# One third of a batch transposed on TensorE instead of by DMA, and a new order of loads and work in a fused attention and GEGLU kernel

## The chip, the cores and the metric

The kernel runs on one core of a Trainium2 chip. Its time is the device time of one execution in microseconds (us). Three executions of the kernel before took 412.22, 412.31 and 412.85 us; the median, 412.31 us, is the time before. A core has the engines TensorE (PE: matrix products; its weight loads are listed as PEld), VectorE (DVE), ScalarE (ACT), GpSimd (POOL) and SyncE (SP), each with its own queue of instructions that is worked off in order. POOL and SP issue transfers (DMAs), which 16 DMA engines carry out.

## The reference

Attention without softmax, then a gated feed-forward block, in float32:

```python
batch, n_heads, seq, head_dim = (8, 12, 448, 64)
scores = scale * np.matmul(q, k.transpose(0, 1, 3, 2))
attn = np.maximum(scores, 0.0) ** 2 / S
attn_out = np.matmul(attn, v)
x = attn_out.transpose(0, 2, 1, 3).reshape(B * S, H * D)     # 3584 x 768
g, val = x @ w_gate, x @ w_val                               # 768 -> 1536
gelu = 0.5 * g * (1.0 + erf(g * inv_sqrt2))
out = gelu * val @ w_out                                     # 1536 -> 768
```

## The kernel before, in words

The eight batches are numbered 0 to 7, so the third batch is number 2. A batch's 12 heads are worked in three thirds of four heads (two pairs of heads); the third m of batch b is written (b, m) here and in the code.

**Loads.** POOL issues all loads, and they turn float32 into bf16 on the way. A third of q and one of k go into one tile `qk16` (from a ring of two buffers), a third of v, in two overlapping halves, into `v16` (a ring of three). The gate and value weights come in six column blocks each, `wg[i]` and `wv[i]` (`load_w12`, L410), the output weights in four row blocks `wo[i]` (`load_wo`, L417). A load into a ring waits until the old contents of its buffer have been used. Since POOL issues in order, a load that waits holds all those behind it. In the built program a load also waits for the landing of the one eight places before it, with whose completion semaphore it shares a number. Loads of later batches have one more wait: for a relu instruction of an earlier third (`PACE`, "behind"). In the kernel before, the order of loads is written out as calls at the end of the function: batch 0; weight block 0; third (1, 0); then blocks 1 to 5 between the other thirds of batch 1; then q and k of (2, 0) and (2, 1), v of (2, 0), all four blocks of `wo`, and the remaining thirds, v one third behind q and k.

**Transposes.** The scores need q and k with the head dimension on the partitions (tile `qkT`, a ring of three). For batches 0 and 1 TensorE transposes them with an identity matrix into PSUM (`add_transposes`, products `<-ident,qk` at L641, 28 for each third) and DVE copies the result to `qkT` (two copies, L645). For batches from 2 on (`EARLY = 2`), DVE regroups the third into a tile `qkr` (L477, a ring of two) and SP issues two DMA transposes of `qkr` into `qkT` (L482). Some of these wait for the landing of the one before.

**Attention and feed-forward.** A score unit multiplies into PSUM, ACT applies relu (L708), DVE squares two units at once (L717), and a value unit of each head pair multiplies with v into `xT`. For batches 0 and 1 and some blocks of the others, gate and value products are plain: ACT takes the Gelu (L1002), DVE multiplies (L1007). For blocks 0 to 2 of later batches, two batches together are computed with seven products in place of eight (Winograd's form), and so is the output product, with sums of weights (`ws`, `wt`) and of tokens made on DVE. Nearly all products of TensorE are of 64 x 64 tiles, of which four run beside each other, issued by one helper (L375).

**The order.** The work of TensorE after the first batch is a list of units, named by the string `LINE`: `s` is the next score (or transpose) unit, `o` the next value unit, a digit the next gate or value unit of that batch, `2B4` a product of a pair of batches, `g2` one of the output's groups. At build time `run_plan` plays through all engines with assumed costs: at each step it takes, from the next 60 units of the list, the one that can start first; ACT, DVE and SP take what is ready first. The instructions are emitted in this order, so every engine's order is fixed when the kernel is built. The plan knows when a load lands by adding sizes over an assumed rate; it gives every DMA transpose a landing 5 us after its issue.

Of the kernel before, what the change touches and what calls it, by code (L numbers as in the profile page):

```python
# [9 lines left out]


LINE = """
0 1 4A1 s 1 s 1 0 o 2 5 1 1 o d1 s 4C5 1 1 1 0 o 0 0 c5 s 2C1 s s o 3 s 0 s a1 s 0 1 2B4 o 5 2 g2
o s 3 0 2 b7 s 1 o 6B6 o s s s a5 a7 s 4B1 2 d4 s 0 0 0 0 o s 0 a2 4D1 2C7 s s s o 2E1 2A5 0 2C6 s
2A6 0 0 0 0 b5 0 s s 2 0 s 1 0 s s 1 a6 4E5 d7 2B1 2E2 1 0 o g6 1 f1 s 1 a4 c4 s s 4A2 1 b6 s s
2B6 s s 1 2D3 s o s s o d3 o c2 6B1 s s s 1 s s s 1 b2 s s b1 s s 1 s 3 1 s 2D6 1 c7 a3 s s 2E3 o
f5 o o 2E6 1 g7 1 2F1 b4 s 2B2 s 2A3 b3 2B3 c1 s o s 2F2 4 s s i5 3 c3 4F5 s s c6 s 2 2E7 2C3 2
2B5 2D1 s s 2F3 e6 2B7 s s s 2 3 2 s 2A1 2 6F4 g4 2A2 s 2A7 4E4 s 2A4 s o s s 4 e4 3 o d5 s s o
2D7 2D4 4A5 2C5 o 2D2 s o h2 2C2 2F6 s 2F7 2E5 s 5 f6 2D5 j2 2 4 4A4 4F6 s s 2C4 2F5 e2 s s 5 s
2F4 o 3 o 3 6B5 2E4 h4 2 s 4C1 m6 3 s 3 d6 s 6B2 s 4 3 s s n2 f3 f4 s o d2 o 3 4B4 4A7 6E1 s s e1  # L20
6B7 e7 o o 4B3 g1 s 7 4 6D6 s o f2 s e3 s 6E3 s 5 e5 s 4 6D3 7 m3 4D4 4E7 s m4 f7 s s 4 m5 4A6 s s
5 4 4B6 s 4B2 s s g5 i1 4C2 o o s s 4D2 4 4 s j5 s s j3 j1 s 6C6 g3 5 i7 6 s k5 6A2 o 4B7 s 4F2 5
4D5 4C6 4E2 4E1 s s 4B5 4A3 s s 4D3 s 4E6 6C7 4C3 s 6C3 o 4F3 6A1 4C7 s 4D6 s n1 l4 o s 6A7 s 4 k3
4C4 6 s o h1 4E3 i3 4D7 s h7 6A6 6E7 6 i4 s 4F1 j6 6 o 4 4F4 s n3 s 5 4F7 s i6 s s n5 s s 6D1 6 s
5 h6 s 5 o s 6A5 7 7 6D2 o s s 5 s h5 l7 6 s s 6C4 s n7 s 6E4 6A3 s o 6C1 6E6 i2 o 6E2 7 j7 7 s h3
l5 s s s 6B3 s l1 j4 s 7 6F2 6 s 6C2 k6 o k7 6 6F1 6D7 m7 6B4 7 6A4 6 6 m1 6F7 6 n6 6F6 k4 l2 6E5
m2 l6 k1 6 6D4 7 7 l3 7 7 6C5 6F3 6D5 6F5 n4 k2
"""


class Op:

    def __init__(self, engine, cost, emit, deps=(), lag=0.0, prio=0, other=None):
        self.engine, self.cost, self.emit, self.prio = engine, cost, emit, prio
        self.deps = [d for d in deps if d is not None]
        self.lag = lag
        self.other = other
        self.takes = None
        self.margin = 0.0
        self.after = None  # L40
        self.gates = []
        self.start = self.end = None
        self.place = 0
        self.open = False

# [45 lines left out]
AHEAD = 60  # L91
BANK = 0.3
SPARE = 1


def run_plan(queues, pools, units, banks, arrivals, together, fill):

    free = {e: 0.0 for e in (*queues, *pools)}
    at = {e: 0 for e in queues}
    dma = last = floor = busy = 0.0  # L100
# [11 lines left out]
        for d in before:  # L112
            users.setdefault(d, []).append(op)
    able = {e: [] for e in pools}
    known = {}

    def offer(op):
        t = 0.0 if op.after is None else op.after.start
# [20 lines left out]

    def ready(op):  # L140
        t = known.get(op)
        if t is not None and op.takes is not None:
            x = op.takes[0].free(*op.takes[2:])
            return None if x is None else max(t, x)
        return t
# [63 lines left out]
    while left:  # L209
        best = None  # L210
        for e, ops in queues.items():
            if at[e] < len(ops):
                r = ready(ops[at[e]])
                if r is not None:
                    t = max(r, free[e], floor if e in together else 0.0)
# [23 lines left out]
        if isinstance(op, tuple):  # L239
            _, u, k = op  # L240
# [16 lines left out]
            op = u.los[0]  # L257
# [10 lines left out]
        if op in arrivals:  # L268
            dma = max(dma, op.end) + arrivals[op]
            op.lag = dma + 2.0 - op.end  # L270
        if e in at:
            at[e] += 1
        else:
            for x in homes[op]:
                able[x].remove(op)
# [13 lines left out]
def kernel(  # L289
# [18 lines left out]
    SC = S // P  # L308
    VC = (SC + 1) // 2
    NPAIR = H // 2  # L310
    NM = NPAIR // 2
# [11 lines left out]
    WOG = 3  # L323
# [2 lines left out]
    FB = 4  # L326
    FILL = 30.0
    EARLY = 2
    WO_AT = 2, 2, 2, 2

    NP = 3
    RING_V, RING_T, RING_H, RING_L, RING_A, RING_O, RING_E = 3, 3, 2, 2, 4, 4, 5
# [49 lines left out]
    ACT, DVE, POOL, SP, IDLE = [], [], [], [], []  # L382
    arrivals = {}
# [22 lines left out]
    def load_w12(i):  # L406
        cols = slice(i * WCH, (i + 1) * WCH)

        def emit(wt, src):
            return nc.gpsimd.dma_start(  # L410
                wt[:, :, :], src[:, cols].rearrange("(c p) f -> p c f", p=128))
        w12_op[i] = [load(4 * d_model * WCH, lambda wt=wt, src=src: emit(wt, src))
                     for wt, src in ((wg[i], moe_w_gate), (wv[i], moe_w_val))]

    def load_wo(i):
        rows = slice(i * WOG * 128, (i + 1) * WOG * 128)
        wo_op[i] = load(4 * WOG * 128 * d_model, lambda: nc.gpsimd.dma_start(  # L417
            wo[i][:, :, :], moe_w_out[rows, :].rearrange("(c p) f -> p c f", p=128)))

    def load_qk(b, i, h0, h1, deps=()):  # L420

# [28 lines left out]
            for pr in range(h0 // 2, h1 // 2):  # L450
                head_op[b, pr, 2 + i] = op

    def load_heads(b, h0, h1):
        load_qk(b, 0, h0, h1)
        load_qk(b, 1, h0, h1)
        load_v(b, h0, h1)

    qkT, tr_op = {}, {}

    def qkT_tile(b, m):  # L460
# [5 lines left out]
    one = []  # L466

    def add_dma_transposes(b, m, deps=()):


        wait = Op("IDLE", 2.0 if b == EARLY else 5.0, lambda: None,
                  [*deps] + [head_op[b, pr, i] for pr in (2 * m, 2 * m + 1) for i in range(2)])
        IDLE.append(wait)

        def emit_copy():
            qkr[b, m] = lpool.tile([128, SC, 4, D], bf16, name="qkr", tag="qkr")
            nc.vector.tensor_copy(  # L477
                qkr[b, m].rearrange("p c h d -> p h c d"),
                qk16[b, m].rearrange("p h (c d) -> p h c d", d=D))

        def emit_transpose(c0, c1):
            ins = nc.sync.dma_start_transpose(  # L482
                qkT_tile(b, m)[:, c0:c1].rearrange("d c r x -> d (c r) x"),
                qkr[b, m][:, c0:c1].rearrange("p c h d -> p (c h d)"))
            if b > EARLY and c0 or m and b == EARLY:
                tc.add_manual_dep(ins.ins, one[0].ins.name, SYNC, reason="pace")
            one[:] = [ins]

        n = len(regrouped)
        copy = Op("DVE", 0.62, emit_copy, [wait, *(regrouped[n - RING_L] if n >= RING_L else ())], lag=0.15, prio=1)  # L490
        DVE.append(copy)
        copy.margin = 3.0
        tr_op[b, m] = [Op("SP", 0.19 * 2 * (c1 - c0), lambda c0=c0, c1=c1: emit_transpose(c0, c1),
                          [copy], lag=5.0) for c0, c1 in ((0, VC), (VC, SC))]
        qk_used[b, m] = [copy]
        t_made[b, m] = [*tr_op[b, m]]
        if m or b > EARLY:
            tr_op[b, m][1].deps.append(tr_op[b, m][0])
        if m and b == EARLY:
# [171 lines left out]
    def add_scores(at, b, u):  # L671
# [44 lines left out]
            part = slice(u % 2, u % 2 + 1) if alone else slice(0, 2)  # L716
            nc.vector.tensor_tensor(a[:, part], a[:, part], a[:, part], op=ALU.mult)  # L717

        if b < EARLY:
            have = [t for pr in prs for t in ([t_op[b, m, pr % 2]] if (b, pr) != (0, 0) else t_op[0, 0])]  # L720
        else:
            have = tr_op[b, m]
# [516 lines left out]
        if h0 > 2:  # L1239
            load_v(0, h0 - 4, h1 - 4)  # L1240
    load_v(0, 8, 12)
    load_w12(0)
    load_heads(1, 0, 4)
    load_w12(1)
    load_qk(1, 0, 4, 8)
    load_qk(1, 1, 4, 8)
    load_w12(2)
    load_v(1, 4, 8)
    load_qk(1, 0, 8, 12)
    load_qk(1, 1, 8, 12)  # L1250
    load_w12(3)
    load_v(1, 8, 12)
    load_w12(4)
    load_w12(5)
    late = [(b, m) for b in range(2, B) for m in range(NM)]
    for n, (b, m) in enumerate(late):
        for i in range(FC // WOG):
            if WO_AT[i] == n:
                load_wo(i)
        for i in range(2):  # L1260
            load_qk(b, i, 4 * m, 4 * m + 4)
        for b_, m_ in late[n - 1:n] + (late[n:] if n == len(late) - 1 else []):
            load_v(b_, 4 * m_, 4 * m_ + 4)
    add_weight_sums()
    for b, m in late:
        add_dma_transposes(b, m)


    FINAL = B * SC // 4 - 1
# [199 lines left out]
```

## Time and profile before

The profiled execution took 411.88 us, 0.43 us under the median; its span from the first to the last instruction is 410.1 us.

| what | profiled execution before |
|---|---|
| time, span | 411.88 us, 410.1 us |
| PE busy, products | 392.3 us (96%), 8477 |
| DVE busy | 298.5 us (73%) |
| ACT busy | 244.8 us (60%) |
| POOL busy | 74.1 us (18%) |
| mean granted clock of TensorE | 0.985 |
| DMA: loads' queue, SP's queue (share of 16 engines) | 46.3%, 24.1% |
| DMA transposes | 36, 5.3 us to landing (median) |

Busy time of PE is the time in which any product runs; with four tiles beside each other a busy PE need not be a full one. A wait's line names the waiting group, what ended the wait, the total, the number and the longest of the waits. A line of the timeline gives start, duration, engine, source line, operation, names, shapes and count. The windows give busy time of PE, PEld, DVE, ACT and POOL with counts, then the granted clock (1.00 is full), the mean share of the 16 DMA engines and GB/s.

### The profile page before, as it was taken

How to read it: one execution, taken by the hardware profiler on the slowest of the kernel's cores; microseconds unless marked ns; L12 is line 12 of the kernel's file. 1: busy time of each engine (PE TensorE's matmuls, PEld its weight loads, DVE VectorE, ACT ScalarE, POOL GpSimd, SP SyncE). 2: the span in 40 equal slices, each digit the busy share in tenths (PEclk: the TensorE clock that was granted, in tenths of full speed). 3: DMA queues.
4: the chain of work that ended last, by engine and by line, in shares of the span. 5: the costliest groups of instructions: out<-in, count | busy, mean ns of one | idle time of the engine just before them, and what ended most of it. 6: DMA issues, size and time to landing. Idle time of an engine off the chain costs nothing.

```text
span 410.1 us, 18547 instructions
## 1 busy us (share of the span) xinstructions
PE 392.3 (96%) x8477; PEld 348.1 (85%) x8480; DVE 298.5 (73%) x513; ACT 244.8 (60%) x366; POOL 74.1 (18%) x120
## 2 busy tenths in 40 slices
PE   7999996499999999999999999999999999999994
PEld 3566785399989899989998999999999999989993
DVE  2976776198677978788877777688998766577562
ACT  5947783167677667786666676677776733242220
POOL 7756350111212211110111111111110000000000
PEclk9999999599999999999999999999999999999999
DMA  8999999987899799636498987765331411000245
GB/s 108 190 200 197 198 206 180 122 103 105 131 124 136 119 192 154 93 49 71 56 136 127 158 169 116 122 63 81 54 48 42 118 42 40 4 3 3 65 113 136
DMA packets 75278, 44.84 MB, mean 109 GB/s; under 512 B 36160, under 2 KB 71744, under 8 KB 75200
## 3 DMA queue, kind: packets, MB, share of 16 engines
q0 software_dynamic: 37152, 24.39, 46.3%
q1 hardware_dynamic: 37888, 19.08, 24.1%
q8 instruction: 66, 1.08, 1.1%
q10 hardware_dynamic: 160, 0.20, 0.1%
q14 instruction: 12, 0.10, 0.1%
HBM read 48.76 MB, written 11.01 MB: 146 GB/s over the span
## 4 chain that ended last, share of the span: by engine, by line
PE 91%; DMA 5%; ACT 1%; issue 1%; DVE 1%; SPq 0%; POOL 0%; POOLq 0%
PE ff L375 80%; PE sp L375 8%; DMA qkT<-qkr 4%; PE ff L562 1%; ACT attnT L708 1%; PE sp L641 1%; DMA qk<-in_k_dram 1%; PE ff L641 0%; DVE qkT L645 0%; DVE attnT L717 0%; PE ff L604 0%; ACT gel L1002 0%; DVE osb L1196 0%; SPq L482 0%; ACT qkT L612 0%
## 5 line engine op out<-in xcount | busy, mean ns | idle before, releaser
L375 PE MATMUL ff<-xT,wg 64*64 64x448 bf16 x1872 | 195.4, 351 | 0.0
L708 ACT ACTIVATE attnT<-sp 128x896 bf16<-128x896 f32 x168 | 151.6, 922 | 55.8 <-PE sp L375 53.4
L375 PE MATMUL ff<-xT,wv 64*64 64x448 bf16 x1440 | 156.3, 352 | 0.2 <-issue 0.2
L375 PEld LDWEIGHTS <-wv 64*64 64x64 bf16 x1872 | 115.3, 107 | 8.6 <-issue 0.9
L375 PEld LDWEIGHTS <-wg 64*64 64x64 bf16 x1872 | 113.7, 107 | 9.0 <-issue 0.2
L717 DVE TENSOR_TENSOR attnT<-attnT 128x1792 bf16<-128x1792 bf16 (+1 forms) x98 | 92.3, 953 | 12.6 <-ACT attnT L708 11.9
L375 PE MATMUL sp<-qkT 64*64 64x448 bf16 (+1 forms) x768 | 79.7, 330 | 10.1 <-DMA qkT<-qkr 9.0
L375 PEld LDWEIGHTS <-s 64*64 64x64 bf16 x1344 | 80.2, 107 | 4.4
L375 PE MATMUL ff<-attnT,v 64*64 64x448 bf16 (+1 forms) x768 | 83.7, 326 | 0.1
L375 PE MATMUL ff<-wo,s 64*64 64x384 bf16 x672 | 60.9, 323 | 0.0
L375 PE MATMUL ff<-wt,s 64*64 64x384 bf16 x672 | 60.8, 323 | 0.0
L1007 DVE TENSOR_TENSOR uT<-gel,ff 128x448 bf16<-128x448 bf16 x60 | 37.0, 617 | 31.2 <-PE ff L375 27.0
L375 PEld LDWEIGHTS <-uT 64*64 64x64 bf16 x912 | 55.2, 107 | 2.1
L375 PEld LDWEIGHTS <-qkT 64*64 64x64 bf16 x768 | 39.4, 106 | 16.5 <-issue 7.5
L445 POOL DMA_DIRECT2D v<-in_v_dram x48 | 29.5, 619 | 128.6 <-ACT attnT L708 98.2
L375 PE MATMUL ff<-ts,wv 64*64 64x448 bf16 x432 | 51.5, 349 | 0.0
L375 PE MATMUL ff<-ts,ws 64*64 64x448 bf16 x432 | 51.1, 349 | 0.0
L375 PEld LDWEIGHTS <-v 64*64 64x64 bf16 x768 | 46.9, 106 | 4.0 <-issue 1.0
L375 PE MATMUL ff<-wo,uT 64*64 64x384 bf16 x576 | 49.9, 323 | 0.0
L1002 ACT ACTIVATE gel<-ff 128x448 bf16<-128x448 f32 x60 | 32.5, 544 | 27.0 <-PE ff L375 26.9
L375 PEld LDWEIGHTS <-ws 64*64 64x64 bf16 x648 | 41.1, 106 | 2.3
L924 DVE TENSOR_TENSOR part<-ff,part 128x448 f32<-128x448 f32 x54 | 32.9, 620 | 11.8 <-PE ff L375 7.0
(60 smaller groups left out, 374.7 us busy)
## 6 DMA issues: line engine op xcount, KB each, us to landing
out_dram<-osb SPq DMA_DIRECT2D x54, 192.0 KB, 3.6
v<-in_v_dram POOLq DMA_DIRECT2D x48, 128.0 KB, 3.9
qk<-in_q_dram POOLq DMA_DIRECT2D x23, 224.0 KB, 4.9
qk<-in_k_dram POOLq DMA_DIRECT2D x23, 224.0 KB, 5.9
wg<-in_moe_w_gate_dram POOLq DMA_DIRECT2D x6, 384.0 KB, 10.3
wv<-in_moe_w_val_dram POOLq DMA_DIRECT2D x6, 384.0 KB, 11.2
wo<-in_moe_w_out_dram POOLq DMA_DIRECT2D x4, 576.0 KB, 13.5
qkT<-qkr SPq DMA_TRANSPOSE x36, 5.3
```

The lines of the kernel that those rows point to most:

```text
L375: return nc.tensor.matmul(o, lhsT, rhs, start=start, stop=stop, skip_group_check=onto, tile_position=(P * row, P * col))
L445: return nc.gpsimd.dma_start(v16[b, m][HALF[i], :, :, :], v[b, h0:h1].rearrange("h (p c) d -> p h c d", c=SC)[:, :, c0:c0 + VC, :])
L562: nc.tensor.matmul(t[:, :], warm[:, 0:128], warm[:, :], start=True, stop=True)
L641: nc.tensor.transpose(t[HALF[j], c, :], src[:, 2 * r + j, c, :], ident[:, :], tile_position=(0, P * j))
L708: relu.ins = nc.scalar.activation(duo["a"][:, u % 2, :, :], box[0][:, :, 0:S], AF.Relu).ins
L717: nc.vector.tensor_tensor(a[:, part], a[:, part], a[:, part], op=ALU.mult)
L924: rd.ins = nc.vector.tensor_tensor(t[:, :], box[0][:, 0:S], t[:, :], op=ALU.add).ins
L1002: nc.scalar.activation(gel[b, fc][:, :], box[0][:, 0:S], AF.Gelu)
L1007: u_op[b, fc].ins = nc.vector.tensor_tensor(uT[b][:, fc, :], gel.pop((b, fc))[:, :], box[0][:, 0:S], op=ALU.mult).ins
```

## The change

Three things change, and the order of nearly everything with them.

1. The third (2, 0) is transposed on TensorE (`ON_PE`): 28 more products with the identity and two DVE copies out of PSUM; one `qkr` copy and two DMA transposes less. The others of batch 2 and all later ones stay with DMA.
2. The loads follow a string `LOADS`. After batch 0 it has q, k and v of (1, 0) before weight block 0, then q and k of (1, 1), block 1, v of (1, 1), all of (1, 2), q and k of (2, 0), blocks 2 and 3, q and k of (2, 1), block 4, `wo[0]`, q and k of (2, 2) and (3, 0), v of (2, 0), (2, 1) and (2, 2), block 5, v of (3, 0), and so on; `wo` comes as 0, 2, 1, 3, spread out.
3. `LINE` is a new list. The plan's assumptions change too: rates of the weight loads, at most eight loads in flight (`FLIGHT`), and the time that a DMA transpose takes of the DMA engines (`queued`). These act only at build time, through the order.

```diff
 LINE = """
-0 1 4A1 s 1 s 1 0 o 2 5 1 1 o d1 s 4C5 1 1 1 0 o 0 0 c5 s 2C1 s s o 3 s 0 s a1 s 0 1 2B4 o 5 2 g2
...
+2 2B1 0 f1 s s s 2C4 b1 2F1 4D4 0 1 o 0 1 4D3 h2 f5 s 2 o 4D5 o 1 0 s o s s b7 s 3 4B3 0 2B6 1 s s
...
+LOADS = """
+q v w q w v q v q w w q w o q q v v v w v q o o q o q v q v v q v v q q q q v v v q v q v q v q v
+q v v
+"""
...
+FLIGHT = 8
...
-    known = {}
+    known, landed = {}, []
...
         t = known.get(op)
+        if t is not None and op in arrivals and len(landed) >= FLIGHT:
+            t = max(t, landed[-FLIGHT])
...
             op.lag = dma + 2.0 - op.end
+            landed.append(op.end + op.lag)
+        elif op.queued:
+            dma = max(dma, op.end) + op.queued
+            op.lag = dma + 2.0 - op.end
...
-    WO_AT = 2, 2, 2, 2
+    ON_PE = ((2, 0),)
...
-            if b > EARLY and c0 or m and b == EARLY:
+            if one and (b > EARLY and c0 or m and b == EARLY):
...
+        for op, n in zip(tr_op[b, m], (VC, SC - VC)):
+            op.queued = 0.75 * n
...
-        if b < EARLY:
+        if b < EARLY or (b, m) in ON_PE:
...
-    load_w12(0)
-    load_heads(1, 0, 4)
-    load_w12(1)
...
+    todo = {"w": [*range(NW)], "o": [0, 2, 1, 3], "q": [(1, m) for m in range(NM)] + late,
+            "v": [(1, m) for m in range(NM)] + late}
+    for x in LOADS.split():
+        n, at = len(POOL), todo[x].pop(0)
+        if x == "w":
+            load_w12(at)
+        elif x == "o":
+            load_wo(at)
+        elif x == "v":
+            load_v(at[0], 4 * at[1], 4 * at[1] + 4)
+        else:
+            for i in range(2):
+                load_qk(at[0], i, 4 * at[1], 4 * at[1] + 4)
...
     for b, m in late:
-        add_dma_transposes(b, m)
+        if (b, m) not in ON_PE:
+            add_dma_transposes(b, m)
...
-            if b < EARLY and u in (0, SC):
-                work.append((LATER, 1, add_transposes, (b, u // SC + 1, (0, 1))))
+            for m in [0] * (u == 0 and b > 1) + [u // SC + 1] * (u in (0, SC)):
+                if b < EARLY or (b, m) in ON_PE:
+                    work.append((LATER, 1, add_transposes, (b, m, (0, 1))))
```

In the built program the products of TensorE go from 8480 to 8508 and the DMA transposes from 36 to 34; the first DMA transposes are now those of (2, 1).

More of the change, by code (lines that the diff above doesn't have):

```diff
@@ L12 @@
 LINE = """
-0 1 4A1 s 1 s 1 0 o 2 5 1 1 o d1 s 4C5 1 1 1 0 o 0 0 c5 s 2C1 s s o 3 s 0 s a1 s 0 1 2B4 o 5 2 g2
[L14 to L27, printed above, removed]
+2 2B1 0 f1 s s s 2C4 b1 2F1 4D4 0 1 o 0 1 4D3 h2 f5 s 2 o 4D5 o 1 0 s o s s b7 s 3 4B3 0 2B6 1 s s
+o s 2A4 s s o 0 3 2A5 a6 0 b6 5 s 6B7 s 4C1 a3 1 1 1 a7 s s 0 0 s s s 0 s s a1 3 s s 0 0 2 s 0 s o
@@ new lines @@
+c6 2C5 0 s 2A7 1 1 s 0 o 0 o o 2F7 2A3 0 i4 s 0 6E3 1 s 2B2 1 0 1 b2 1 s s 2 s s a2 s a4 s c5 s 1
+s 1 s a5 0 o 0 s s s 6 2 o b5 1 0 s 1 1 1 2F6 2 s s s 2 1 2 c7 o s 1 o 1 c2 e6 1 s o s 1 2F3 k5 s
+s 2D3 2E5 s 6B1 c1 s 2C1 s b3 2B4 o 2C7 s 6 s s g3 s 2B3 b4 6D6 c4 d4 o o s s s s s 2 s f4 g1 s
+2A1 e3 2A6 2C3 n1 i1 2C6 2E1 o s d5 s 2 2B7 s 3 5 4D7 s s 2A2 s s 2D1 2E4 s 2D4 2C2 d3 e1 c3 5 o
+4B1 g5 o 2D7 s s 2B5 2D2 2D5 o s 2F2 d7 3 2F4 2 7 2D6 s d6 s s 4C2 2E2 2E7 f7 s 2 o 3 2E6 e2 s s s
+4F7 o 6F1 2E3 h5 4 7 s 4B4 n2 3 s 4A1 o s e7 s s 4A2 2F5 o 3 s 4D1 s 4 4A5 o o 4B6 s o s f3 3 e5
@@ new lines @@
+d1 s 3 s 3 m1 g4 d2 s o l5 s 3 o 4E7 g7 s e4 6D2 s j3 4D6 f2 s s 4A4 f6 s s g6 s 4C7 s 4A3 o 5 s s
+s o g2 s s 4F1 5 5 i5 7 s 4 4D2 s 4 4B2 6F2 7 j4 s 6 4E4 6A7 s 6B5 4E2 s 6B6 l6 4 s 4A6 i3 4A7 6C6
+4E3 4 4B7 4 6E6 4F5 6 s h1 4 5 4C6 s l3 s 6 5 4C4 4B5 s 4 6A3 4E5 6E1 4C5 s 4C3 s s s 4 6D1 o 4F6
+4E6 s s o s 4F3 s 4E1 4 6C5 4 5 6A1 4F4 h4 s 6B4 4F2 o s s s m4 6B2 6D3 k4 s s 5 s o s 5 h7 6 s k6
+o j5 5 i6 6D7 s j1 6A2 o s s 6A5 m6 6C1 i2 j6 h6 h3 6E2 i7 6F4 o s n5 6 s 6C7 s j2 s s s l1 6 6E4
+6D5 7 s 6E5 s o 6A6 s 6C2 s 6 6F7 j7 6B3 s m2 6 7 6C3 l2 o 6E7 6 m7 6F6 6 n7 k3 l7 l4 7 k7 m5 7 k1
@@ L28 @@
+7 6A4 7 6C4 6D4 7 7 k2 m3 n3 6F3 6F5 n6 n4
+"""
+LOADS = """
+q v w q w v q v q w w q w o q q v v v w v q o o q o q v q v v q v v q q q q v v v q v q v q v q v
+q v v
 """
@@ L42, in __init__ @@
         self.start = self.end = None
+        self.queued = 0.0
         self.place = 0
@@ L411, in emit @@
                 wt[:, :, :], src[:, cols].rearrange("(c p) f -> p c f", p=128))
-        w12_op[i] = [load(4 * d_model * WCH, lambda wt=wt, src=src: emit(wt, src))
+        w12_op[i] = [load(4 * d_model * WCH, lambda wt=wt, src=src: emit(wt, src), rate=385e3)
                      for wt, src in ((wg[i], moe_w_gate), (wv[i], moe_w_val))]
@@ L417, in load_wo @@
         wo_op[i] = load(4 * WOG * 128 * d_model, lambda: nc.gpsimd.dma_start(
-            wo[i][:, :, :], moe_w_out[rows, :].rearrange("(c p) f -> p c f", p=128)))
+            wo[i][:, :, :], moe_w_out[rows, :].rearrange("(c p) f -> p c f", p=128)), rate=410e3)
     def load_qk(b, i, h0, h1, deps=()):
@@ L451, in load_v @@
                 head_op[b, pr, 2 + i] = op
[L453 to L456, printed above, removed]
     qkT, tr_op = {}, {}
@@ L498, in add_dma_transposes @@
             tr_op[b, m][1].deps.append(tr_op[b, m][0])
-        if m and b == EARLY:
+        if m and b == EARLY and (b, m - 1) in tr_op:
             tr_op[b, m][0].deps.append(tr_op[b, m - 1][1])
@@ L1241 @@
     load_v(0, 8, 12)
-    load_w12(0)
-    load_heads(1, 0, 4)
-    load_w12(1)
[L1245 to L1254, printed above, removed]
-    late = [(b, m) for b in range(2, B) for m in range(NM)]
[L1256 to L1263, printed above, removed]
+    late = [(b, m) for b in range(2, B) for m in range(NM)]
+    todo = {"w": [*range(NW)], "o": [0, 2, 1, 3], "q": [(1, m) for m in range(NM)] + late,
[11 more added lines that the diff above has]
+                load_qk(at[0], i, 4 * at[1], 4 * at[1] + 4)
+        for op in POOL[n:]:
+            op.token = x, at
+    assert not any(todo.values())
     add_weight_sums()
     for b, m in late:
-        add_dma_transposes(b, m)
+        if (b, m) not in ON_PE:
+            add_dma_transposes(b, m)
     FINAL = B * SC // 4 - 1
```

## The prediction

> **What bounds the kernel now.** I read the page first. PE is busy 96% of the span, but its row over the 40 slices has one hole, and the granted clock drops there.
>
> ```profile
> PE   7999996499999999999999999999999999999994
> PEclk9999999599999999999999999999999999999999
> ```
>
> So after the first 25 us this is a kernel bound by PE with one stop in it. Then I asked what PE waited for, longest first:
>
> ```profile
> PE sp L375 <- DMA qkT<-qkr: 9.0, 1, 9.0
> PE ff L1376 <- DVE table L364: 1.2, 1, 1.2
> ```
>
> One wait of 9.0 us, by a score product, for a DMA transpose; all others together are 3 us, most of it the start. The windows around it (PE, PEld, DVE, ACT, POOL busy; clock; DMA share; GB/s):
>
> ```profile
> 60.00:65.00 5.00, 5.00 (x115) 4.37 (x111) 3.74 (x6) 3.14 (x5) 1.13 (x2) 1.00 1.17 184
> 65.00:70.00 5.00, 3.52 (x76) 2.82 (x69) 3.14 (x8) 1.52 (x3) 0.00 (x0) 1.00 1.22 187
> 70.00:75.00 5.00, 0.00 (x0) 0.12 (x1) 0.56 (x1) 0.00 (x0) 0.00 (x0) 0.55 1.24 173
> 75.00:80.00 5.00, 2.47 (x28) 1.56 (x31) 0.00 (x0) 1.73 (x2) 0.61 (x1) 0.50 0.74 104
> 80.00:85.00 5.00, 5.00 (x106) 4.20 (x101) 4.16 (x7) 2.24 (x4) 0.61 (x1) 0.92 1.00 122
> ```
>
> PE stops at 68.5 us, starts again at 77.5 and runs at half clock until about 80.8: 2.47 us at 0.50 lose 1.2, and 5.00 at 0.92 lose 0.4. The stop costs 9.0 + 1.6 = 10.6 us. Meanwhile the DMA engines are full. The chain of waits, in order of time, names the transfer:
>
> ```profile
> 57.64 0.55 ACT gel L1002
> ...
> 59.01 0.53 SPq L482
> 59.54 0.04 issue
> 59.58 17.90 DMA qkT<-qkr
> 77.48 0.04 issue
> 77.53 0.96 PE sp L375 x7
> ```
>
> This is the second transpose of (2, 0): 17.9 us, where the median of all 36 is 5.3. Ahead of it POOL had issued all four `wo` loads (52.0 to 55.4 us), which took up to 18.0 us to land, and loads issued just behind took 16 to 17.6. Between 62 and 72 us the loads' queue moved 1069 packets and SP's queue 1057, so the two took turns. [...]
>
> **The change part by part.**
>
> *The stop goes: -10.6.* The first third on DMA is now (2, 1), and it must have room. I count products of TensorE in the built order between the work that the regrouping copy stands behind and the first score with the tile, at 24 products a us (236 to 246 in the 10 us windows at 120, 200 and 300 us). Before, (2, 0) had 286 products, 11.9 us, and needed 20.0 (copy at 57.48, second landing at 77.48): short by 8, about the stop. In the new order (2, 1) has 483, 20.1 us; (2, 2) has 447, 18.6; (3, 0) has 596, 24.8; later ones 20 us or more from their copy, but for one second half with about 13 from its issue, against a landing of 5.3 median. Even the slow 20.0 us would just fit for (2, 1), and its neighbours are lighter: one `wo` load in place of four. I take no wait; bounds 0 and 2 (20.0 against 18.6 for (2, 2), plus PE starting late).
>
> *28 transposing products: +1.0.* For the same work on batch 1 the timeline has:
>
> ```profile
> 26.84 0.97 PE L641 MATMUL sp<-ident,qk 128*64 128x128 bf16 x28
> 27.74 0.76 PE L375 MATMUL ff<-xT,wg 64*64 64x448 bf16 x6
> ```
>
> The next product starts 0.90 us after the first of them; in two batches of 14 at 32.27 and 33.28 it is 0.51 each. PE is the bound there, so this is on the path: 1.0.
>
> *Two copies from PSUM on DVE (0.62 each), one `qkr` copy less (0.62): 0 to +0.6.* DVE is busy 3.1 to 4.8 of 5 us there. But the first score of (2, 0) stands only 21 products (0.9 us) behind the last transposing one and waits for the first copy: 0.2 until it starts, as elsewhere, and 0.62, if DVE is then free. Should it be in the middle of another instruction (0.6), PE waits that long. I take +0.2. The transposes also take a turn in the scores' PSUM, so they wait for a relu; the score unit in their place would have done so too.
>
> *Weights behind (1, 0): +0.3, between 0 and +3.* In this stage the loads land one behind the other: a block of `wg` or `wv` every 2.0 us, a q or k third every 1.1, half a v third every 0.7. The last load of batch 0 lands at 17.8 (issued 11.03, 6.8 to landing), unchanged. Then come q, k and v of (1, 0): 2.2 + 1.4, to 21.4; `wg0` lands at 23.4 and `wv0` at 25.4, against 19.8 and 21.8 before. The first `wg` product ran at 24.78, after ACT's chain of relus for batch 0, so 1.4 us are left. `wv` ran from 25.37 between the last value products; the built order now puts it behind them, about 25.9, so 0.5 are left, but those gaps go unfilled: the six `wv` products that ran in them are 6/24 = 0.25, say 0.3. POOL's issues keep up: v of (1, 0) waits for the same PE work as before (issued at 17.64), `wg0` and `wv0` follow at 18.9 and 19.7. `wg2` comes behind 13.4 us of loads more, at 40.8; the product with as much PE work ahead of it ran at 42.9 before. Later blocks have more room. The upper end is `wg2` and `wv0` each 1.5 us later than so reckoned.
>
> *POOL's queue: 0, up to +4.* `q` and `k` of (2, 2) need the buffer that the copy of (2, 1) frees, so POOL stands still behind `wo[0]`, from about 43 us (`wo[0]` may go once `wg2` has landed) to about 54 (the PE work ahead of that copy was done at 50 before, and squares stand between), and so do v of batch 2 and block 5 behind it. Next, k of (3, 0) waits for a relu of (2, 0); v of (2, 0) follows, with 193 products (8.0 us) from that relu's scores to its first use. It needs 0.2 + 0.92 (relu) + 0.62 + 0.63 (two issues) + 4.5 (longest landing of a v load, 80 to 100 us) = 6.9. `wg5` has 197 products, 8.2 us, and needs 0.2 + 0.92 + 0.63 + about 5.5 (2.0 of transfer, 3.2 as the shortest landing, some sharing) = 7.3. One us is left in each; I take 0.
>
> *`wo` spread out: 0, up to +2.* The last blocks are needed some 15 us of PE work or more after what releases their issue; the worst landing of a `wo` load was 18.0 with four in a row, now at most two. DVE's sums of them may wait 1 us; nothing behind them is urgent. The ends of both orders are alike (the same last groups of output products).
>
> Sum: 411.88 - 10.6 + 1.0 + 0.2 + 0.3 = 402.8 for a profiled execution like this one. That one was 0.43 below the median of the runs, so I give 403.2.
>
> **The rivals.**
>
> *A, the thin places give.* v of (2, 0), `wg5` or (2, 2) come 1 to 5 us late. For: margins of one us worked out from medians. Against: a lighter DMA queue. 404.5 to 409; middle 406.5.
>
> *B, slower: POOL's queue makes the new stop.* v of (2, 0) lands as the loads did beside transposes, 17.6 us after issue in place of 4.5. Then PE waits 2.4 + 17.6 - 8.0 = 12.0 us at its first use, and pays the half clock again: 403.2 + 12.0 + 1.6 = 416.8. It becomes slower than before once that landing exceeds about 14 us. For: transposes of (2, 2) are issued at that time. Against: the slow landings stood behind four `wo` loads; here POOL has been waiting, so the queue is nearly empty.
>
> *C, the early stage starves.* `wv0`, q and k of (1, 1) or `wg2` land late and PE has nothing else in its fixed order: 2 to 4 us, 405 to 407.
>
> *D, the clock.* More transposing products could let the clock fall: half a clock for 3.3 us as at 77.5 costs 1.6, 404.8. Against: it was 1.00 in all windows from 25 to 45 us, which hold 84 of them. [...]
>
> **How the numbers follow.** The forecast gets 0.61, A 0.17, B 0.08, C 0.07, D 0.02; 0.05 is for gains and waits that cancel by chance or a new order that is better still. A measurement of this kernel can tell about 0.2% (0.8 us) from no change. Faster: the forecast, A, C, D and part of the rest, 0.89; same 0.02; slower 0.09. The forecast's own range is 401.5 to 405. The range reaches into A: 401.0 to 408.5; B and the worst of A are out.
>
> **What would show it.** PE's waits should hold no DMA transpose over 1 us, and the clock should stay at 1.00 from 10 us on. `<-ident,qk` products go up by 28, with about 1 us of PE for them near 58 us. The (2, 1) transposes are issued around 54 us and land within 20. If there is a wait for `v`, `wg` or `wv` of 2 us or more, A, B or C is right, and its start tells which: about 72 us, about 79, or under 45. The prediction is wrong if the hole in PE's row moves instead of going.

## The result, and the profile after

Four executions of the changed kernel took 409.62, 406.53, 413.24 and 414.61 us, those of the kernel before beside them 411.98 to 412.85. The ratio is 0.9896, with a 95% interval of 0.9865 to 0.9927: about 4.3 us faster, where 9.1 were forecast. The ratios, here and in the table of the experiments, leave out executions that lie far above the fastest of their kernel, here the two above 413 us, and the medians leave out none: the median of all four is 411.43 us, so the ratio flatters the changed kernel, to which such executions seem to belong (see the count of the half clock below).

The profiled execution took 409.62 us (span 407.8), 2.26 less than the one before. PE's row and the granted clock over the 40 slices, in the page of after:

```profile
PE   7989999899999999999999999999999999999994
...
PEclk9999999989999999999999999999999999999999
```

The hole at 68 to 78 us is gone. Its place is taken by two dents, in slice 3 (20 to 31 us) and slice 8 (71 to 82 us). The waits of PE in after, longest first:

```profile
PE ff L388 <- issue: 2.6, 2, 2.0
PE ff L1383 <- DVE table L377: 1.2, 1, 1.2
PE ff L388 <- DMA wg<-in_moe_w_gate_dram: 0.7, 1, 0.7
PE ff L388 <- DMA wv<-in_moe_w_val_dram: 0.6, 1, 0.6
```

No DMA transpose holds up PE any more. The first line is new: 2.0 us at one go in which PE waited for nothing that the profile shows ("issue"). Windows of after (PE, PEld, DVE, ACT, POOL busy; clock; DMA share; GB/s):

```profile
25.00:30.00 5.00, 3.60 (x46) 1.79 (x40) 2.44 (x5) 1.16 (x2) 1.25 (x2) 1.00 1.34 192
...
75.00:80.00 5.00, 4.58 (x98) 3.58 (x89) 3.47 (x6) 3.05 (x5) 1.07 (x2) 1.00 1.55 132
80.00:85.00 5.00, 3.37 (x40) 2.75 (x44) 1.06 (x1) 1.35 (x2) 0.00 (x0) 0.68 1.42 186
```

PE loses 1.4 us at 25 to 30 (before: 4.94 busy), and from 79.6 to 85.2 a stop and 3.4 us of half clock. PE's timeline in after at that stop (start, duration, products):

```profile
79.23 0.35 PE L388 MATMUL ff<-xT,wv 64*64 64x448 bf16 x1
81.63 0.50 PE L388 MATMUL ff<-xT,wv 64*64 64x448 bf16 x1 [2.04 <-issue]
```

To see where time goes I set each product's start against the work of PE ahead of it, each product counted as long as it takes at full clock with four tiles beside each other. What it has lost is its lateness; the table gives how much is added in each stretch of that work, worked out from the traces ("alone" is the experiment with (2, 0) on TensorE alone):

| stretch of PE's work | before | after | alone |
|---|---|---|---|
| up to 7 us | 6.7 | 7.9 | 8.0 |
| 7 to 28 us | 6.7 | 8.9 | 6.7 |
| 28 to 48 us | 0.8 | 1.1 | 0.8 |
| 48 to 65 us | 11.1 | 4.3 | 1.8 |
| 65 us to the last products | 7.7 | 7.3 | 7.4 |
| work at the same last product | 371.3 | 372.1 | 372.1 |

In the stretch of the old stop after gains 6.8 us, not some 10, because a new stop stands there; it loses 2.2 us at 7 to 28 us of work and 1.2 at the start.

What came late at 79.6? The trace shows TensorE's instructions arriving on a DMA queue of their own, q8, in blocks of 16384 bytes: 66 of them in before and in after, for the 16,988 and 17,042 instructions of TensorE in the two traces, so one block for each 256, or 128 weight loads with their products. Queues of after at 70.1 to 79.0 us, then at 79.0 to 80.3 (q0 has the loads, q1 what SP issues; packets, MB, share of 16 engines):

```profile
q0 software_dynamic: 1575, 0.85, 89.9%
q1 hardware_dynamic: 1056, 0.26, 51.3%
```

```profile
q0 software_dynamic: 488, 0.24, 136.4%
q8 instruction: 1, 0.02, 5.6%
```

Between 70.1 and 79.0 us no block came at all; the next ran from 79.02 to 80.18. Blocks usually come 5 to 6.5 us apart (in after the middle half of the 65 distances is 4.9 to 6.5), this one 9.9 us behind the last. That is theory 1: loads and transposes held up the instructions, and PE ran out of them. Its rival, theory 2: a late load (v of batch 2, or block 5, which landed at 83 and 86 us) made the stop by a wait that the profile doesn't show.

### The profile page after: what moved, and what is told of

It is laid out like the page before. It is cut to its first block, busy times and chain, and to the rows that moved or that the text cites. A ratio compares the mean times of both kernels' runs of the same rounds, so it can differ in the third digit from the quotient of the medians.

```text
span 407.8 us, 18581 instructions
## 1 busy us (share of the span) xinstructions
PE 395.3 (97%) x8505; PEld 345.9 (85%) x8508; DVE 299.2 (73%) x514; ACT 244.0 (60%) x366; POOL 74.0 (18%) x120
## 4 chain that ended last, share of the span: by engine, by line
PE 95%; DMA 2%; issue 1%; POOL 0%; DVE 0%; ACT 0%
PE ff L388 83%; PE sp L388 8%; DMA wv<-in_moe_w_val_dram 2%; PE sp L651 1%; PE ff L1383 1%; PE ff L572 1%; PE ff L651 1%; POOL v L458 0%; PE ff L614 0%; DVE osb L1206 0%; ACT qkT L622 0%; DVE held L374 0%; POOL wg L423 0%; DVE table L377 0%
## 5 line engine op out<-in xcount | busy, mean ns | idle before, releaser
L388 PE MATMUL ff<-xT,wv 64*64 64x448 bf16 x1440 | 158.4, 351 | 2.7 <-issue 2.0
L388 PE MATMUL ff<-attnT,v 64*64 64x448 bf16 (+1 forms) x768 | 85.6, 330 | 0.1
L388 PEld LDWEIGHTS <-s 64*64 64x64 bf16 x1344 | 77.8, 107 | 3.5
L388 PEld LDWEIGHTS <-uT 64*64 64x64 bf16 x912 | 53.8, 107 | 2.5 <-issue 0.7
L388 PE MATMUL ff<-wt,s 64*64 64x384 bf16 x672 | 52.6, 323 | 0.0
L388 PE MATMUL ff<-wo,uT 64*64 64x384 bf16 x576 | 52.4, 323 | 0.0
L388 PEld LDWEIGHTS <-v 64*64 64x64 bf16 x768 | 48.4, 108 | 3.8 <-issue 0.6
L458 POOL DMA_DIRECT2D v<-in_v_dram x48 | 29.8, 628 | 99.2 <-ACT attnT L718 80.3
L388 PEld LDWEIGHTS <-qkT 64*64 64x64 bf16 x768 | 37.6, 107 | 7.7 <-issue 4.0
L388 PEld LDWEIGHTS <-ws 64*64 64x64 bf16 x648 | 39.7, 106 | 3.3
```

What stands on the lines that cost most here:

```text
L388: return nc.tensor.matmul(o, lhsT, rhs, start=start, stop=stop, skip_group_check=onto, tile_position=(P * row, P * col))
L458: return nc.gpsimd.dma_start(v16[b, m][HALF[i], :, :, :], v[b, h0:h1].rearrange("h (p c) d -> p h c d", c=SC)[:, :, c0:c0 + VC, :])
```

## The experiments

All ratios are to runs of the kernel before on the same chip; the medians of these on the three chips used were 412.70, 412.75 and 413.02 us.

| run | median us (executions) | ratio, 95% interval |
|---|---|---|
| after_again | 408.75 (10) | 0.9909, 0.9873 to 0.9945 |
| shift_96 | 411.77 (12) | 0.9963, 0.9932 to 0.9994 |
| shift_224 | 409.68 (12) | 0.9882, 0.9850 to 0.9913 |
| block5_early | 410.59 (12) | 0.9917, 0.9883 to 0.9951 |
| block0_early | 406.78 (5) | 0.9850, 0.9818 to 0.9882 |
| block0_again | 406.08 (6) | 0.9836, 0.9812 to 0.9859 |
| blocks05_early | 408.56 (5) | 0.9904, 0.9882 to 0.9927 |
| pe_alone | 404.54 (5) | 0.9805, 0.9782 to 0.9828 |
| pe_shift_96 | 404.78 (5) | 0.9799, 0.9776 to 0.9821 |
| pe_block0_late | 407.29 (6) | 0.9845, 0.9818 to 0.9873 |
| old_weights | 411.53 (12) | 0.9966, 0.9943 to 0.9988 |
| extra_traffic | 413.44 (12) | 1.0029, 1.0012 to 1.0047 |

### Late instructions or late loads: the place of the stops

The changed kernel again, two kernels with more warm-up products, and block 5 earlier on POOL:

```diff
-        for _ in range(8):
+        for i in range(8 * n):                     # n = 4 or 8, each 512 / n columns
             for j in range(2):
-                nc.tensor.matmul(t[HALF[j], :], warm[:, HALF[j]], warm[:, :],
+                nc.tensor.matmul(t[HALF[j], part], warm[:, HALF[j]], warm[:, part],
```

```diff
 POOL's loads (block5_early):
+wg[5] wv[5]
 wo[0], q k (2,2), q k (3,0), v (2,0), v (2,1), v (2,2)
-wg[5] wv[5]
 v (3,0), ...
```

> The changed kernel, unaltered, once more, as the measure for the other runs and for its own spread. In its profiled execution TensorE stood idle from 79.58 to 81.63 us, and the granted clock was 0.5 until 85.16. Theory 1 (late instructions): TensorE had used up its instructions, because a block of 16384 bytes on queue q8 came at 79.02, 9.9 us after the one before where 5 to 6.5 are usual. How long such a block is held up depends on what the DMA engines have in hand at that moment, so the stop should be there in most executions, but of another length, and times between 406 and 415 are expected. Theory 2 (late loads): a load of block 5 or of v ends the stop; then the stop should repeat with the same length, as it did in the kernel before, and the times should lie within 1 us of 409.6.

> The 16 warm-up products of 512 columns at the start become 64 of 128 columns: the same columns in all, 96 more instructions of TensorE, nothing else changed. After 96 more instructions each block of instructions is asked for 96 instructions earlier in the work, about 2.0 us at 128 instructions in 2.7 us. Theory 1 (late instructions): the stop at 79.6 us changes its place or size. If it goes, 409.6 - 4.1 = 405.5 us; if the block asked for 2 us earlier meets the same transfers it is at least not the same stop. Theory 2 (late loads): nothing changes, 409.6 with an idle time of 2.0 us at 79.6 and the half clock behind it.

> As the run with 64 products, but 128 warm-up products of 64 columns: 224 more instructions, seven eighths of a block of 256. Each block is asked for 32 instructions, 0.7 us, later in the work than another block was in the changed kernel. Theory 1: the stop stays at about its place and is as long or up to 0.7 us longer, 409.6 to 411. Theory 2: nothing changes, 409.6. Taken with the run with 96 more instructions it tells whether the place of the blocks in the work matters or only the number of warm-up products.

> The two loads of gate and value weights of block 5 are issued just ahead of wo[0], into POOL's idle time of 47 to 57 us; every other engine keeps its order. This takes 4.0 us of loads (2.0 for each) out of 74 to 86 us, where they ran beside the transposes of (2, 2). Theory 1 (late instructions): the DMA engines have less in hand at 73 to 79 us, the block of instructions is held up by 4 us or less as elsewhere, and the stop of 2.0 us with its half clock goes: 409.6 - 4.1 = 405.5. Theory 2 (late loads): if block 5 ended the stop, also 405.5; if it was v of (2, 1) or (2, 2), a part of it goes, 407 to 408. If the transposes alone hold up the instructions, the stop stays: 409.6.

In the profiled executions of after, of these four runs and of four later ones I took every idle time of PE over 0.35 us that stands without any wait on a semaphore, and counted the instructions of TensorE that had run (weight loads, products and the 29 to 32 waiting ones between them). The profiles of before, pe_alone, pe_shift_96 and old_weights have no such stop:

```
run              stops: at us (length), instructions run = blocks of 256 + rest
after            79.6 (2.0) 10 + 191;  187.3 (0.5) 28 + 191
after_again      54.1 (0.5) 5 + 190;  84.6 (1.7) 10 + 191;  92.6 (2.1) 11 + 191
shift_96         106.3 (0.8) 15 + 191;  112.8 (1.3) 16 + 191;  130.6 (1.9) 19 + 191;  234.3 (1.0) 37 + 190
shift_224        85.7 (0.7) 12 + 191;  115.2 (0.7) 17 + 191;  201.9 (0.7) 32 + 190
block5_early     113.8 (1.6) 16 + 191
blocks05_early   65.4 (1.4) 8 + 193;  72.9 (2.0) 9 + 193;  98.6 (0.7) 13 + 193;  116.7 (1.3) 16 + 194
block0_again     77.2 (1.0) 10 + 194;  84.2 (1.0) 11 + 194;  114.1 (2.2) 16 + 194;  185.2 (1.0) 28 + 194
pe_block0_late   155.0 (1.3) 23 + 194
extra_traffic    240.4 (0.6) 37 + 194
```

All 23 stops stand at the same place, 190 to 194 instructions above a multiple of 256 (three product records are missing where it is 190 or 191). One place picked at random would be among these five of 256 in 2 of 100 cases. In the shifted kernels the extra instructions are in the count, so the same rest is another place in the work: the work at which after stopped (10 + 191) is at 11 + 31 with 96 more, and nothing stopped there. Late loads would have kept the place in the work. Theory 2 falls, and with it my expectation for shift_224 that the stop stays where it was. The time did not follow any one stop: shift_96 lost its stop at 79.6 and got four others, and its median is 3 us above the changed kernel's. block5_early had a good profiled execution, 405.78 us, as expected, but a median of 410.59: moving block 5 alone settles nothing. Late loads do cost something near this place all the same: in shift_96 a wait of 0.9 us for `wg[5]` ends at 81.2 us, in shift_224 one of 0.3 at 81.0.

The executions after_again spread from 406.97 to 414.88, pe_alone from 403.67 to 404.84. The profiled execution of after_again was the slowest and shows a second cause. Its windows:

```profile
25.00:30.00 5.00, 3.76 (x40) 1.56 (x35) 2.02 (x4) 0.74 (x1) 1.09 (x2) 0.88 1.34 195
30.00:35.00 5.00, 5.00 (x58) 3.10 (x58) 1.78 (x3) 0.00 (x0) 2.46 (x4) 0.50 1.43 196
35.00:40.00 5.00, 5.00 (x70) 2.62 (x70) 1.16 (x2) 1.27 (x2) 2.44 (x4) 0.59 1.10 148
```

PE waited 1.2 us for `wv[0]` until 28.45, and then ran at half clock from 28.82 to 39.06, 10.24 us, 58 products in a window that holds 94 to 104 in after, shift_96, shift_224 and block5_early. So the early wait cost some 5 us more than itself there, by 10.24 us at 0.50.

### The early stage: block 0 of the weights

```diff
 POOL's loads:
+wg[0] wv[0]
 q k (1,0), v (1,0)
-wg[0] wv[0]
 q k (1,1), wg[1] wv[1], ...
```

> The changed kernel with the two loads of gate and value weights of block 0 issued ahead of q, k and v of (1, 0), as in the kernel before; nothing else moves. Theory E (early stage): in the changed kernel TensorE waits 0.6 to 1.2 us each for wg[0] and wv[0] at 26 to 29 us, because the loads' queue runs dry while POOL waits for the buffers of (1, 0); in one execution this stop was followed by 10.24 us of half clock. Then both waits go, about 2 us are gained against the changed kernel's 408.75 (406.5 to 407), and executions above 411 us become rare unless late instructions cause them. Rival: q, k and v of (1, 0) now land 4 us later, TensorE waits for them instead, and nothing is gained: 408 to 409.

> The changed kernel with block 0 ahead of (1, 0) once more, for a profile at full clock: no wait for wg or wv over 0.2 us before 30 us, 406 to 407.5; what it has above 404.5 are stops without a wait at 190 to 194 above a multiple of 256 instructions, about 2 us in sum, after 60 us. If there are no such stops, the rest lies elsewhere in the new order of units.

The reverse edit in the kernel with (2, 0) on TensorE alone:

> The kernel before with (2, 0) on TensorE (404.5 us), and block 0 issued behind q, k and v of (1, 0), as the change has it; no other engine's order changes. Theory E: the waits for wg[0] and wv[0] of 0.6 to 1.2 us appear at 25 to 29 us, and the time rises by 1.4 to 2.2 us, to 406 to 406.7; in some executions the stop is followed by 10.24 us of half clock, another 5 us, near 411. Rival: the order of block 0 costs only together with the changed units; then 404.5.

With block 0 first, the changed kernel goes from 408.75 to 406.78 and 406.08. With block 0 late, the other kernel goes from 404.54 to 407.29. Some of the intervals in the table touch; the waits and windows settle it. The waits of block0_again hold none for `wg` or `wv`, and PE is busy at 25 to 30 us again:

```profile
25.00:30.00 5.00, 4.95 (x90) 3.08 (x85) 3.70 (x7) 0.64 (x1) 2.20 (x4) 1.00 1.39 198
```

Waits of pe_block0_late:

```profile
PE ff L400 <- issue: 1.6, 2, 1.3
PE ff L400 <- DMA wv<-in_moe_w_val_dram: 1.2, 1, 1.2
...
PE ff L400 <- DMA wg<-in_moe_w_gate_dram: 0.7, 1, 0.7
```

The waits are there, 0.7 and 1.2 us as expected (the 1.3 us in the first line is the instruction stop at 155 us in the list above). The same window without and with the edit, first pe_alone, then pe_block0_late:

```profile
25.00:30.00 5.00, 4.89 (x90) 3.10 (x85) 4.01 (x8) 1.27 (x2) 2.40 (x4) 1.00 1.38 199
```

```profile
25.00:30.00 5.00, 2.94 (x43) 1.39 (x38) 2.30 (x5) 1.01 (x2) 2.36 (x4) 1.00 1.42 191
```

PE loses 2 us there. By the lateness of the table above, 9.5 us are added at 7 to 28 us of work with block 0 late and 6.7 without; in the changed order it is 8.9 in after and 6.8 in block0_again. The half clock follows the same edit: of 56 executions with block 0 late (after, after_again, both shifts, block5_early, pe_block0_late) 16 had a mean clock of 0.986 or less, and they were on average 1.8 to 5.9 us slower than the others of their kernel; of 25 with block 0 early (block0_early without its profiled execution of 688 us, block0_again, blocks05_early, pe_alone, pe_shift_96) none had. Only one of the 16 was profiled, so that the half clock of all stands at 29 us is inferred from this count. Half clock came behind other waits too: old_weights below has block 0 early, and 5 of its 12 executions were at 0.986 or less, the profiled one with half clock behind waits at 30 and 80 us. block0_early has no profile but that of the 688 us, so block0_again stands for it.

### One part alone: (2, 0) on TensorE in the old order

```diff
+    ON_PE = ((2, 0),)
...
-        if b < EARLY:
+        if b < EARLY or (b, m) in ON_PE:
             have = ...
...
-        add_dma_transposes(b, m)
+        if (b, m) not in ON_PE:
+            add_dma_transposes(b, m)
```

`LINE` and the order of loads stay those of the kernel before, with the new transposing unit three units ahead of the first score of (2, 0); a list of numbers in the kernel fixes the order of the units.

> The kernel before with one part of the change alone: (2, 0) transposed on TensorE, in the kernel before's own order of loads and units (the 28 transposing products are put three units ahead of the first score of (2, 0)). By the sum of the prediction, with no cost for weights behind (1, 0): 412.3 - 10.6 + 1.0 = 402.7 us. Theory 1 (late instructions): the 9.0 us stop of the kernel before came while the DMA engines were full, and let no instructions be used; without it the blocks asked for at 65 to 80 us, beside four wo loads and the transposes of (2, 1), come late: one or two stops without a wait, 0.5 to 2 us each, at 190 or 191 above a multiple of 256, with up to 3.4 us of half clock: 404 to 407. A rival: the transposes of (2, 1) land as late as those of (2, 0) did, 17.9 us after issue, and the wait is back for (2, 1): 409 or more.

> The kernel before with (2, 0) on TensorE, and the 16 warm-up products split into 64 of 128 columns: 96 more instructions, the same columns. Theory 1: the largest hold-up of a block there was 4.4 us, under the 5.3 us at which TensorE stops, so another place of the blocks costs little: 404 to 405.5, at most one short stop. If that kernel only had a lucky place of its blocks, stops of 1 to 2 us come, and 406 to 409.

404.54 us, 0.9805 of before: the first part alone gains twice what the whole change does, and beats both kernels. Waits of pe_alone:

```profile
PE ff L666 <- DMA qk<-in_k_dram: 1.9, 2, 1.4
PE ff L1403 <- DVE table L389: 1.2, 1, 1.2
```

Both are in the first 12 us. The four `wo` loads and (2, 1) crowd as before; its transposes are issued at 62.50 and 75.52, and land 13.0 and 5.0 us later, but no product waits for them. My expectation of one or two instruction stops was wrong: the longest hold-up (below) of a block at 50 to 120 us was 4.2 us, and no idle time without a wait passed 0.35 us. The longest, 0.26 us at 71.8, stands at 9 + 193, so the same thing happens here, but costs little. Nor was that a lucky place of the blocks: with 96 more instructions 404.78 us, and again no stop over 0.35 us. The 5.3 us at which TensorE was to stop was an estimate of mine; by the hold-ups below gaps came from 3 us on.

### What of the new order makes the stops

> The changed kernel with block 0 issued ahead of (1, 0) and block 5 issued ahead of wo[0]. By theory 1 (late instructions) and theory E together both losses shrink: 409.6 - 4.1 - 2.0 = 403.5 us for a profiled execution; what stops are left stand without any wait where the number of TensorE instructions (weight loads and products) is 190 or 191 above a multiple of 256, as all such stops did in the five executions seen so far, and at different places in the work. If the stops come from the loads, none is left at all.

> The changed kernel's order on TensorE, DVE, ACT and SP, but the weights are issued where the kernel before had them: block 0 ahead of (1, 0), blocks 1 to 5 between the thirds of batch 1 with blocks 4 and 5 ahead of q of (2, 0), and the four wo loads together ahead of q of (2, 2). q, k and v stay in the changed kernel's order. If the new order of the weight loads makes the stops for late instructions (more traffic left for 65 to 120 us, beside the transposes), they go, as does the wait for block 0: 404 to 405 us with little spread, as with the transposes of (2, 0) on TensorE alone (404.5). If the new order of units makes them, they stay: 406 to 409 and stops of 0.5 to 2 us at 190 to 194 above a multiple of 256 instructions. A third way: block 5 and wo come too early for POOL, which then issues v of (2, 0) late, and TensorE waits for it.

`old_weights` puts all weights where the kernel before had them:

```diff
 POOL's loads:
-... q k v (1,0), w0, q k (1,1), w1, v (1,1), q k v (1,2), q k (2,0), w2, w3, q k (2,1), w4, wo[0], q k (2,2), ...
+... w0, q k v (1,0), w1, q k (1,1), w2, v (1,1), q k (1,2), w3, v (1,2), w4, w5, q k (2,0), q k (2,1), wo[0..3], q k (2,2), ...
```

blocks05_early missed: 408.56 with four stops (the list above), 1.8 to 2.5 us more than with block 0 alone. Two improvements to loads did not add up; that the second moved traffic, so that other blocks came late, fits the list but was not tested by itself. The profiled execution of block0_again, 1.8 us above its median, has almost as much, where I had expected about 2 us:

```profile
PE ff L388 <- issue: 5.1, 4, 2.2
```

old_weights went the third way. Its waits:

```profile
PE sp L388 <- DMA qkT<-qkr: 2.7, 1, 2.7
PE sp L673 <- DMA qk<-in_k_dram: 2.4, 1, 2.4
PE ff L388 <- DMA v<-in_v_dram: 1.5, 1, 1.5
```

There is no instruction stop, but the new list of units reaches a transposing unit at 30 us, v of (2, 0) at 77 and a transposed third at 80, before their transfers are in, and half clock follows twice, 3.41 us from 33.4 and 6.83 from 81.2: 411.53. So the new units need the new order of loads, or most of it, and the two together leave more loads for the time when blocks are due. At 65 to 120 us the loads' queue moves 4.9 to 5.9 MB in the seven profiles of after and its variants (old_weights apart), 4.3 to 4.8 in old_weights, pe_alone, pe_shift_96 and pe_block0_late. The median hold-up of a block at 50 to 120 us is 2.9 to 4.5 us in the seven, 1.9 and 2.0 in pe_alone and pe_shift_96; but it is 2.6 in old_weights and 2.8 in pe_block0_late, with the old units, so that the units and the loads are not cleanly told apart. Which packets make 6 us of hold-up where others make 4 stays open.

### Traffic by itself

> The kernel before, with five loads (3 of 786 KB and 2 of 524 KB, from the gate weights) and four DMA transposes added behind the last relu of (7, 2), where the DMA engines are nearly idle. Their results go to free buffers that nothing reads, and no engine's order changes. In the kernel before the blocks of instructions there start 0.0 to 1.5 us after the 182nd instruction ahead of them has run. Theory 1 (DMA traffic holds up the instructions): beside the extra traffic this becomes 3 to 6 us, and if it passes 5.3 us TensorE stops, without a wait, at 190 or 191 above a multiple of 256: 0 to 3 stops, 0 to +4 us. If it is something else in the busy stage (the number of instructions in flight, the other engines), the delays there stay under 1.5 us and the time stays at 412.

```diff
+    held_up = relus[B - 1, NM - 1, SC - 1]
+    # five loads of moe_w_gate into free buffers, four dma_start_transpose of the last qkr
```

Windows of before at 330 to 345 us, then of extra_traffic:

```profile
330.00:335.00 5.00, 5.00 (x117) 4.48 (x109) 3.80 (x7) 0.87 (x2) 0.00 (x0) 1.00 0.10 23
335.00:340.00 5.00, 5.00 (x117) 4.72 (x113) 2.25 (x4) 2.22 (x5) 0.00 (x0) 1.00 0.32 83
340.00:345.00 5.00, 5.00 (x112) 4.73 (x107) 3.20 (x6) 2.92 (x6) 0.00 (x0) 1.00 0.23 61
```

```profile
330.00:335.00 5.00, 5.00 (x119) 4.54 (x114) 3.31 (x6) 0.77 (x2) 1.66 (x4) 1.00 1.07 191
335.00:340.00 5.00, 5.00 (x116) 4.65 (x113) 2.69 (x5) 2.56 (x5) 0.00 (x0) 1.00 1.10 198
340.00:345.00 5.00, 4.94 (x108) 4.11 (x102) 3.56 (x6) 1.65 (x3) 0.00 (x0) 1.00 1.18 220
```

I call hold-up the time from when a block is asked for, taken as 185 instructions above a multiple of 256 (the least at which any block moved was 172 to 191, by profile), to when it starts to move. The three blocks that came beside the extra traffic were held up by 3.4, 4.2 and 1.7 us; in before those of 325 to 345 us by 0.0 to 0.7. The second was followed by 0.41 us between two starts in PE's stream of weight loads and products, and PE ran dry for 0.06 us at 344.5, without a wait, at 55 + 194: a stop at the place of all others, if a very short one, made by transfers that nothing waits for. So the loads and transposes together lengthen the hold-up; which of the two does it this run doesn't tell. The 5.3 us of my expectation, an estimate, was too high: the first instruction of a block ran 2.2 us after the block began to move at the earliest (2.27 in before, 2.30 in after), and that time has to fit in too. The blocks of the thirteen profiles (all but block0_early's), by hold-up, and how many of them were followed by such a gap of more than 0.3 us at their place, without a wait on a semaphore:

```
hold-up, us      under 1   1 to 2   2 to 3   3 to 4   4 to 5   over 5
blocks               359      191      112      118       31       12
with a gap             0        0        0       16       19        9
```

Over all profiles the hold-up goes with the loads: its median is 0.6 us, and its longest 4.7, where the loads' queue takes under 0.3 of the DMA engines in the 3 us after the block is asked for; with more loads the median is 2.3 and the longest 7.9.

The time of this run, 1.0029 of before (1.2 us), is not explained by these 0.06 us; its profile has a stop of 0.6 us at 240 us, ahead of the extra traffic, besides.

## Why the prediction was wrong

The sign was right, the size was not: 403.2 forecast, 409.6 profiled and 408.75 as the median of ten more. Two steps failed: the weights behind (1, 0), taken at +0.3, and "I take no wait" for the middle of the kernel. The prediction's own sign of being wrong came: the hole in PE's row moved, from 68.5 to 79.6 us, though it shrank.

- **"The stop goes: -10.6", with the products and copies -9.4.** The mechanism held: no wait for a transpose, and the part alone measures -8.2 (412.75 to 404.54). The (2, 1) transposes came later than reckoned (57.3, not 54), and were done after 11.8 us, within the 20. Most of the missing 1.2 us is in the baseline: the profiled execution of before had an early start, 6.7 us late at 7 us of work, where twelve other profiles have 6.9 to 8.0. The stop ended when the transposes landed, 77.48 us, however late PE had been. The profile of extra_traffic, the same program up to there, was 1.3 us later at the start, and its stop was 7.9 us instead of 9.0, with the landing at 77.55. Without the stop the late start counts.
- **"28 transposing products: +1.0" and "copies: +0.2".** Right: 0.75 us of work, and 0.4 (pe_alone) to 0.7 us (after) of lateness.
- **"Weights behind (1, 0): +0.3, between 0 and +3".** This term failed. As a difference of medians it measured 2.0 to 2.7 us in the changed order and 2.8 in the old one, and in 16 of 56 executions the mean clock was lower, by the count above with it. I took the loads to land one behind the other, with `wg0` at 23.4 and `wv0` at 25.4. But POOL waited for the buffers of (1, 0) and issued `wg0` at 20.04, 1.1 us later than reckoned, into a queue that had nearly run dry: all queues moved 75 GB/s at 17 to 18 us, 85 at 20 to 21 and 58 at 22 to 23, where 190 to 199 stand in the full stretches around them. It landed at 26.93, 6.9 us after its issue and not 4.5, `wv0` at 28.98. The sentence "POOL's issues keep up" was the error: the queue ran down while POOL waited, and block 0 ahead had been the work in it (all queues at 20 to 25 us: 200 GB/s in pe_alone, 133 in pe_block0_late). It is rival C's mechanism ("the early stage starves"), which had 0.07.
- **"POOL's queue: 0" and "`wo` spread out: 0", rivals A and B.** In after v of (2, 0) landed at 74.35 and 75.2, in time, and no v, `wg` or `wv` held PE at 72 or 79 us. Their mechanism exists, though: in shift_96 `wg[5]` is 0.9 us late, in old_weights v of (2, 0) 1.5 and a transpose 2.7. The landing beyond which B is slower than before comes out of B's own sum as about 13 us, not 14.
- **The stop that no list held.** "I take no wait" in the middle failed: a stop without a semaphore, 2.0 us and 3.4 of half clock in the profiled execution, 4.1 us in all. I reckoned with waits on semaphores only, and what came late was the instruction stream, for which the sum had no term. That the old stop went is not enough to make such stops: in before PE used up no instructions for 9 us just while the DMA engines were full, yet pe_alone, without that stop, has none over 0.35 us. The stops at 50 to 135 us came only with the new order and its 4.9 to 5.9 MB of loads at 65 to 120 us; that this order makes them is argued from that, not shown by itself.
- **The clock (rival D).** In after it was 1.00 from 10 to 81.7 us, over all transposing products, (2, 0)'s too. In all profiles it fell in an idle time of PE or less than 1 us behind one (before: at 70.52, 2 us into the stop; after: at 81.75, 0.12 behind its end). In old_weights one such fall, at 33.4 us, came behind 2.4 us of idle time, 14 transposing products and six others, so that there the two can't be told apart.

From before's 411.88 us by the table of lateness: +1.2 (start) +2.5 (7 to 48 us: block 0, copies) -6.8 (old stop goes, new one comes) -0.4 (the rest) +0.8 (more work) = 409.2; the last products and stores end 0.4 later, 409.6.

## What to carry to other kernels

When a stop that ends with a transfer goes, ask what it hid: here a start 1.3 us later moved the end of the stop by 0.07 us (extra_traffic). Where loads are moved to a time when the DMA engines are busy, ask also what else comes over these engines: here it was the instruction stream, whose 23 stops stand without any wait on a semaphore. An order of loads is also the stock with which the queue bridges POOL's waits: here block 0, which waits for nothing, was worth 2.0 to 2.8 us ahead of loads that wait for a buffer. A change of several parts should be measured part by part: here one part, (2, 0) on TensorE, is worth 2.0%, and the rest takes half of that back.

## What the runs showed of the hardware

- TensorE's instructions came in 16384-byte blocks, one for each 256 (66 on q8 in before and in after). From 185 above a multiple of 256, where I take a block to be asked for, to some 447, where PE ran dry without it, are some 260 instructions: 5.3 to 6.5 us of work in before and after from 40 us on, stops apart. None of 662 hold-ups under 3 us was followed by a gap over 0.3 us, but 28 of 43 over 4 us were. One execution (block0_again) had 5.1 us of such stops.
- Some short idle times were followed by half clock: 2.04 us at 79.6 in after by 3.41 us of it, 1.2 us at 27.3 in after_again by 10.24, while 2.2 us at 114 in block0_again were followed by none. In the thirteen profiles each stretch of half clock ahead of the last products lasted 3.41, 6.83 or 10.24 us: one, two or three times 3.41.
